# The k maxima of an attention block taken by VectorE block transposes and a DRAM scratch instead of TensorE transposes

## The chip, the cores and the metric

The kernel runs on one core of one Trainium2 chip. The core has a matrix engine (TensorE, "PE" in the profile; its weight loads are the row "PEld"), a vector engine (VectorE, "DVE"), a scalar engine (ScalarE, "ACT"), GpSimd ("POOL"), and SyncE ("SP"), whose queue issues most of the transfers here. The metric is the device time of one execution in microseconds (us), as the median over several runs.

## What is computed

An attention of the softmax-separated kind feeds a two-layer block. `softmax` over the head dimension of q, softmax over the sequence of k, then two products:

```python
# q, k, v: [8 batches, 8 heads, 576, 64] float32
k_s = k - np.max(k, axis=2, keepdims=True)      # maximum over the sequence, one for each (b, h, d)
k_s = np.exp(k_s)
k_s = k_s / (np.sum(k_s, axis=2, keepdims=True) + 1e-09)
kv = np.einsum('bhsd,bhse->bhde', k_s, v)
x = np.einsum('bhsd,bhde->bhse', q_s, kv)       # q_s: the same softmax of q over its last axis
# x as [4608, 512]; w_in [512, 2048], w_out [2048, 512]
h = x @ w_in
r = np.maximum(h, 0.0)
out = (s * (r * r) + b) @ w_out
```

The change bears on `np.max(k, axis=2)`. The sequence lies over the partitions in this kernel, so that maximum goes across partitions.

## The kernel before

The rows of x are worked in nine blocks of 512 (eight batches' first 512 tokens, and a ninth block of the 64 left over of each batch). A block is 16 *steps*, one for each 128 columns of the hidden layer; there are 144. Step t has two halves on TensorE: 12 matmuls of 128x512 that make `h` (`h_parts`, line 600), and 12 that add to the output `acc` (`o_parts`, line 674), in three terms each, since each operand is split in a high and a low part. Between them stand four operations, ACT `r` (620), DVE `r` (621), ACT `gh` (622) and DVE `gl` (613), and the `acc` half of step t-1 is issued after the `h` half of step t (`LAG = 1`).

The attention is worked in 16 *pairs* of two head pairs (256 columns of x), two for each batch. Pairs 0 and 1 serve the first block, and pairs 2 and 3 the second; these four are laid out beside the first 16 steps, with an order worked out by a class of the kernel's own (`Order`). From step 16 on, each block computes the attention of the next batch beside its own steps: pairs 4 to 15, twelve in all. The generator `pair` (line 490) yields 13 times (`STAGES`), and `advance` (line 788) runs so many of its stages at each half step that two pairs are through by step 13 of a block (`UF`). A stage is then run at each half step, beginning half a step into the block; `kv` is the seventh.

In what order an engine takes its instructions is fixed when the program is built, by a list scheduler: it follows estimated durations, transfers included, and gives an engine, among the instructions that it holds ready, the one that stands first in the text. `held()` adds that an instruction may not go ahead of the last `gl` so far. On the chip each engine takes its queue in that fixed order and waits where an operand isn't there. SP's queue is such a queue too: a transfer that waits holds up those behind it.

A pair, in the text's order. `kt`, `qt` and `vt` are the raw k, q and v (`raws[0]`, one buffer, loaded anew by `loads(pr + 1)` when the pair's last reader is through). Of four heads of k, [128, 4, 5, 64], the maximum over the five row groups is taken on DVE (`k_max_2` 461, `k_max_1` 464 and 465) into `m1` [128, 4, 64]. `k_turn` (469) turns it with two TensorE transposes into PSUM (`kT`, tag `sm`, one buffer), `k_top` (472) reduces over the free axis on DVE to `km` [128, 2], and `spread` (476) spreads it back over all partitions with two more TensorE transposes, of a broadcast, into PSUM (`mb`). `k_less` (480) subtracts on DVE and `k_exp` (487, 488) takes the exponential on ACT and clears the unused rows on POOL. Then q's maximum (520), subtraction on POOL (521) and exponential (523); then `heads` (301), 40 small matmuls of k and v into `kv`, and their scaling; then twice normalisation, transposes (546) and product (563), whose result goes to the next block's x.

Of the kernel before, what the change touches and what calls it, by code (L numbers as in the profile page):

```python
# [8 lines left out]
F32 = mybir.dt.float32  # L9
# [5 lines left out]
ALU = mybir.AluOpType  # L15
AX = mybir.AxisListType
# [10 lines left out]
def attention_moe(ctx: ExitStack, tc: tile.TileContext, q, k, v, w_in, w_out, s, b, out):  # L27
    nc = tc.nc
    B, H, S, D = q.shape
    DM, FF = w_in.shape  # L30
    DO = w_out.shape[1]
    P = 128
    NP = H // 2
    NFC = FF // P
    NQ = 4
    LEFT = S - NQ * P
    NT = NQ + 1
    TB = NQ * P
    LAG = 1
    NTMP = 3  # L40
# [11 lines left out]
    work = ctx.enter_context(tc.tile_pool(name="work", bufs=1))  # L52
    small = ctx.enter_context(tc.tile_pool(name="small", bufs=4))
# [3 lines left out]
    dram = ctx.enter_context(tc.tile_pool(name="dram", bufs=1, space=bass.MemoryType.DRAM))  # L57
# [24 lines left out]
    def by_head(t):  # L82
        return t[:, 0:KQ].rearrange("p (h n d) -> p h n d", h=4, d=D)
# [4 lines left out]
    def v_tile(t):  # L88
        return t.rearrange("p (h n e) -> p h n e", h=4, n=NT)
# [16 lines left out]
    def held():  # L106

        return tc.issue_after(gls[-1].ins)
# [184 lines left out]
    def bc(t, shape):  # L293
        return t.unsqueeze(3).to_broadcast(shape)

    def heads(kv, kt, vt):

        for i in range(2):
            for n in range(NT):
                for h in range(2):  # L300
                    nc.tensor.matmul(  # L301
                        kv[h * D:(h + 1) * D, i], kt[:, i, h, n], vt[:, 2 * i + h, n], start=(n == 0), stop=(n == NT - 1)
                    )

    def scales(pr, z, src):

        nc.vector.tensor_scalar(z, src, 1e-9, None, op0=ALU.add)
        nc.vector.reciprocal(z, z)
        zr = small.tile([P, 2, 2], F32, name=f"zr_{pr}", tag="zr")
        nc.vector.tensor_tensor(out=zr, in0=own, in1=z.unsqueeze(2).to_broadcast([P, 2, 2]), op=ALU.mult)  # L310
        return zr

    def blocks(pr, kv, zr):
        kvf = kvfs[pr % 2]
        shape = [P, 2, 2, D]
        nc.vector.tensor_tensor(
            out=kvf, in0=kv.unsqueeze(2).to_broadcast(shape), in1=zr.unsqueeze(3).to_broadcast(shape), op=ALU.mult
        )
        return kvf
# [135 lines left out]
    def k_tiles(pr):  # L455
        m2 = work.tile([P, 4, 2, D], F32, name=f"m2_{pr}", tag="m2")
        m1 = work.tile([P, 4, D], F32, name=f"m1_{pr}", tag="m1")
        return m2, m1, small.tile([P, 2], F32, name=f"km_{pr}", tag="km")

    def k_max_2(kt, m2):  # L460
        nc.vector.tensor_tensor(out=m2, in0=kt[:, :, 0:2], in1=kt[:, :, 2:4], op=ALU.max)

    def k_max_1(kt, m2, m1):
        nc.vector.tensor_tensor(out=m1, in0=m2[:, :, 0], in1=m2[:, :, 1], op=ALU.max)
        nc.vector.tensor_tensor(out=m1[0:LEFT], in0=m1[0:LEFT], in1=kt[0:LEFT, :, NQ], op=ALU.max)

    def k_turn(m1, kT):
        for i in range(2):
            nc.tensor.transpose(kT[:, i * P:(i + 1) * P], m1[:, 2 * i:2 * i + 2].rearrange("p h d -> p (h d)"), ident)

    def k_top(kT, km):
        nc.vector.tensor_reduce(out=km, in_=kT[:, 0:2 * P].rearrange("p (u s) -> p u s", u=2), axis=AX.X, op=ALU.max)

    def spread(km, mb):
        for i in range(2):
            nc.tensor.transpose(mb[:, i * P:(i + 1) * P], km[:, i:i + 1].to_broadcast([P, P]), ident)  # L476
        return mb

    def k_less(kt, mb, i):
        nc.vector.tensor_tensor(  # L480
            out=kt, in0=kt,
            in1=mb[:, i * P:(i + 1) * P].rearrange("p (h d) -> p h d", h=2).unsqueeze(2).to_broadcast([P, 2, NT, D]),
            op=ALU.subtract,
        )

    def k_exp(kt):
        nc.scalar.activation(kt, kt, AF.Exp)  # L487
        nc.gpsimd.memset(kt[LEFT:P, :, NQ], 0.0)

    def pair(pr):  # L490
        us = (2 * pr, 2 * pr + 1)
        bb = us[0] // NP
        kt, qt, vt = tiles.pop(pr)
        kt, qt, vt = by_head(kt), by_head(qt), v_tile(vt)
        kts, qts = [[t[:, 2 * i:2 * i + 2] for i in range(2)] for t in (kt, qt)]

        def sm(n):
            return ps.tile([P, 512], F32, name=f"{n}_{pr}", tag="sm", bufs=1)

        m2, m1, km = k_tiles(pr)  # L500
        with held():
            k_max_2(kt, m2)
        k_max_1(kt, m2, m1)
        yield
        kT = sm("kT")
        k_turn(m1, kT)
        k_top(kT, km)
        yield
        mb = spread(km, sm("mb"))
        for i in range(2):  # L510
            k_less(kts[i], mb, i)
            k_exp(kts[i])
            yield

        qes = []
        for i in range(2):
            u, qt = us[i], qts[i]
            qm = small.tile([P, 2, NT], F32, name=f"qm_{u}", tag="qm")
            with held():
                nc.vector.tensor_reduce(out=qm, in_=qt, axis=AX.X, op=ALU.max)  # L520
            nc.gpsimd.tensor_tensor(out=qt, in0=qt, in1=bc(qm, [P, 2, NT, D]), op=ALU.subtract)  # L521
            qe = work.tile([P, NT, 2, D], F32, name=f"qe_{u}", tag="qe", bufs=2)
            nc.scalar.activation(qe.rearrange("p n h d -> p h n d"), qt, AF.Exp)  # L523
            qes.append(qe)
            yield

        kv = sm("kv")[:, 0:2 * (D + 1)].rearrange("p (u e) -> p u e", u=2)
        heads(kv, kt.rearrange("p (u h) n d -> p u h n d", u=2), vt)
        kvf = blocks(pr, kv[:, :, 0:D], scales(pr, small.tile([P, 2], F32, name=f"z_{pr}", tag="z"), kv[:, :, D]))
        kvhl = work.tile([P, 2, 2, 2 * D], F32R, name=f"kvhl_{pr}", tag="m2")  # L530
        split(kvf.rearrange("p u h d -> p u (h d)"), kvhl[:, 0], kvhl[:, 1], nc.scalar.copy, nc.gpsimd)
        yield
        def normalize(i):
            u, qe = us[i], qes[i]
            qs = small.tile([P, NT, 2], F32, name=f"qs_{u}", tag="qs")
            nc.vector.tensor_reduce(out=qs, in_=qe, axis=AX.X, op=ALU.add)  # L536
            nc.vector.tensor_scalar(qs, qs, 1e-9, None, op0=ALU.add)
            qr = small.tile([P, NT, 2], F32, name=f"qr_{u}", tag="qr")
            nc.vector.reciprocal(qr, qs)  # L539
            nc.gpsimd.tensor_tensor(out=qe, in0=qe, in1=bc(qr, [P, NT, 2, D]), op=ALU.mult)  # L540

        def transpose(i):
            u, qe = us[i], qes[i]
            qT = ps.tile([P, 1024], F32, name=f"qT_{u}", tag="big")
            for n in range(NT):
                nc.tensor.transpose(qT[:, n * P:(n + 1) * P], qe[:, n, :, :].rearrange("p h d -> p (h d)"), ident)  # L546
            qh = work.tile([P, S], F32R, name=f"qh_{u}", tag="qh")
            ql = work.tile([P, S], F32R, name=f"ql_{u}", tag="ql")
            split(qT[:, 0:S], qh, ql, nc.scalar.copy, nc.vector)
            terms = ((kvhl[:, 0, i], qh), (kvhl[:, 0, i], ql), (kvhl[:, 1, i], qh))  # L550
            return terms

        def product(i, terms):
            u = us[i]
            hp = u % NP

            HB = TB // 2
            xh, xl = x_tile(bb)
            xp = ps.tile([P, 2, 512], F32, name=f"xp_{u}", tag="big")
            halves = [xp[:, 0], xp[:, 1]]  # L560
            for a, (t, src) in enumerate(zip(halves, (slice(0, HB), slice(HB, S)))):
                for j, (lhs, rhs) in enumerate(terms):
                    nc.tensor.matmul(  # L563
                        t[:, 0:src.stop - src.start], lhs, rhs[:, src], start=(j == 0), stop=(j == len(terms) - 1)
                    )
                if a == 1:
                    keep_left(u, t[:, HB:HB + LEFT])
            hl = [t[:, hp, :].rearrange("p (a c) -> p a c", a=2) for t in (xh, xl)]
            split(xp[:, :, 0:HB], hl[0], hl[1], nc.scalar.copy, nc.vector)

        for i in range(2):
            normalize(i)
            yield
            t = transpose(i)
            yield
            product(i, t)
            yield
# [121 lines left out]
    NU = B * NP  # L699
    NBLK = B + 1  # L700
    NSTEP = NBLK * NFC
    STAGES = 13
    tiles = {}

    def transfers():
# [74 lines left out]
    def due(t):  # L780

        blk, f = divmod(t, NFC)
        return NP // 2 * STAGES * (blk - 1 + min(1.0, f / UF))

# [54 lines left out]
```

## Time and profile before

| | |
|---|---|
| median of 3 runs | 901.12 us (900.09 to 901.48) |
| the profiled execution | 900.48 us |
| its span, first to last instruction | 898.7 us |
| TensorE busy | 876.0 us, 97% |
| VectorE busy | 459.5 us, 51% |
| ScalarE busy | 357.4 us, 40% |
| GpSimd busy | 83.6 us, 9% |
| granted TensorE clock, mean | 0.997 |
| chain that ended last | TensorE 89%, of it `h` 41%, `acc` 41% |

The times in the rows below are of the profiled execution. It took 1.8 us more than its span, which is the time around the first and the last instruction. A row of an engine is busy time; a matmul's duration includes its way through the array, so that consecutive matmuls overlap, and what one adds to the time is read from the distance of starts. A granted clock of 1.00 is the full 2.4 GHz of TensorE. A wait that ends on another engine's instruction names it behind an arrow.

### The profile page before, as it was taken

To read this page: it belongs to the slowest core of one execution; us is meant where nothing else is said; L and a number is where in the kernel's file an instruction comes from. 1 tells how busy PE (TensorE), PEld (TensorE's weight loads), DVE (VectorE), ACT (ScalarE), POOL (GpSimd) and SP (SyncE) were. 2 spreads that over 40 slices of the span, in tenths; PEclk is the share of its full clock that TensorE was granted. 3 is DMA by queue.
4 is the path that set the end of the run, shared out by engine and by line. 5 is a ranking of instruction groups with operands and counts; after the bars stand their busy time and mean duration, and the time that the engine had idled before them with its cause. 6 is when DMAs were issued, how large, how long until landed. Compare 5 with 4: busy or idle time off the path is not lost.

```text
span 898.7 us, 11364 instructions
## 1 busy us (share of the span) xinstructions
PE 876.0 (97%) x4528; PEld 721.8 (80%) x4528; DVE 459.5 (51%) x723; ACT 357.4 (40%) x564; POOL 83.6 (9%) x110
## 2 busy tenths in 40 slices
PE   4899999999999999999999999999999999999997
PEld 3577778888888888888888888888888888888886
DVE  6999975563364536353636345554545332223222
ACT  5999863342233333242334333333333322222222
POOL 1000001110020202020102002110202100000000
PEclk9999999999999999999999999999999999999999
DMA  9977211303130303030130213031300110001001
GB/s 241 305 258 240 72 39 50 80 5 81 47 80 4 80 19 109 5 80 3 48 79 18 69 47 80 4 80 47 83 4 1 50 47 1 1 1 47 1 1 47
DMA packets 82308, 57.35 MB, mean 64 GB/s; under 512 B 52944, under 2 KB 77520, under 8 KB 82128
## 3 DMA queue, kind: packets, MB, share of 16 engines
q1 hardware_dynamic: 80848, 55.52, 21.7%
q10 hardware_dynamic: 1408, 1.12, 0.4%
q8 instruction: 35, 0.57, 0.3%
q14 instruction: 17, 0.14, 0.1%
HBM read 46.14 MB, written 10.49 MB: 63 GB/s over the span
## 4 chain that ended last, share of the span: by engine, by line
PE 89%; DVE 4%; ACT 3%; DMA 2%; SPq 1%; issue 1%; ACTq 0%; DVEq 0%
PE h L600 41%; PE acc L674 41%; PE xp L563 2%; PE kv L301 2%; PE qT L546 1%; ACT low L202 1%; DMA raw<-in_q_dram 1%; DVE w L225 1%; ACT st L205 1%; DMA k<-in_k_dram 1%; PE xp L443 0%; DMA q<-in_q_dram 0%; ACT r L633 0%; DVE low L218 0%; DVE st L215 0%
## 5 line engine op out<-in xcount | busy, mean ns | idle before, releaser
L600 PE MATMUL h<-x,w 128*128 128x512 f32 x1728 | 428.9, 393 | 2.3 <-ACT r L633 1.6
L600 PEld LDWEIGHTS h<-x,w 128*128 128x128 f32 x1728 | 321.9, 188 | 70.5 <-ACT r L633 3.4
L674 PE MATMUL acc<-w,gh 128*128 128x512 f32 x1152 | 340.6, 392 | 0.0
L674 PEld LDWEIGHTS acc<-w,gh 128*128 128x128 f32 x1152 | 215.1, 188 | 44.3 <-ACT o L687 0.4
L621 DVE SCALAR_TENSOR_TENSOR r<-r,sb 128x512 f32<-128x512 f32 x128 | 102.0, 797 | 277.2 <-ACT r L620 277.1
L674 PE MATMUL acc<-w,gl 128*128 128x512 f32 x576 | 207.7, 392 | 0.5 <-DVE gl L643 0.5
L620 ACT ACTIVATE r<-h 128x512 f32<-128x512 f32 x128 | 76.5, 597 | 302.6 <-PE h L600 293.0
L613 DVE SCALAR_TENSOR_TENSOR gl<-r,sb,gh 128x512 fp32r<-128x512 f32 x132 | 102.6, 777 | 84.6 <-ACT gh L622 84.2
L622 ACT ACTIVATE gh<-r,sb 128x512 fp32r<-128x512 f32 x128 | 92.7, 724 | 94.3 <-DVE r L621 93.6
L674 PEld LDWEIGHTS acc<-w,gl 128*128 128x128 f32 x576 | 108.1, 188 | 23.7 <-DVE gl L643 1.4
L521 POOL TENSOR_TENSOR q<-q,qm 128x640 f32<-128x640 f32 x24 | 30.3, 1262 | 442.6 <-DVE qm L520 441.3
L540 POOL TENSOR_TENSOR qe<-qe,qr 128x640 f32<-128x640 f32 x24 | 30.6, 1275 | 49.2 <-DVE qr L539 45.0
L487 ACT ACTIVATE k<-k 128x640 f32<-128x640 f32 x28 | 20.4, 736 | 20.1 <-DVE k L480 20.1
L523 ACT ACTIVATE qe<-q 128x640 f32<-128x640 f32 x24 | 17.5, 731 | 21.9 <-POOL q L521 21.9
L536 DVE TENSOR_REDUCE qs<-qe 128x10 f32<-128x640 f32 x24 | 19.6, 817 | 12.7 <-ACT qe L523 12.7
L480 DVE TENSOR_TENSOR k<-k,mb 128x640 f32<-128x640 f32 x28 | 21.9, 816 | 7.3 <-PE mb L476 7.3
L102 DVE TENSOR_TENSOR x<-xp,x 128x512 fp32r<-128x512 f32 x24 | 16.6, 690 | 16.9 <-ACT x L101 16.9
L102 DVE TENSOR_TENSOR ql<-qT,qh 128x576 fp32r<-128x576 f32 x24 | 18.2, 757 | 11.6 <-ACT qh L101 11.6
L563 PE MATMUL xp<-qh,kvhl 128*128 128x256 f32 (+1 forms) x96 | 23.4, 297 | 0.0
L101 ACT CAST qh<-qT 128x576 fp32r<-128x576 f32 x24 | 15.4, 641 | 18.7 <-PE qT L546 18.7
L301 PEld LDWEIGHTS kv<-v,k 128*64 128x64 f32 x600 | 19.4, 141 | 4.2 <-issue 2.0
L301 PE MATMUL kv<-v,k 128*64 128x65 f32 (+1 forms) x600 | 21.4, 228 | 0.0
(101 smaller groups left out, 519.8 us busy)
## 6 DMA issues: line engine op xcount, KB each, us to landing
st<-in_moe_w_in_dram SPq DMA_DIRECT2D x16, 512.0 KB, 7.7
st<-in_moe_w_out_dram SPq DMA_DIRECT2D x16, 512.0 KB, 8.5
out_dram<-o SPq DMA_DIRECT2D x16, 512.0 KB, 2.7
q<-in_q_dram SPq DMA_DIRECT2D x14, 512.0 KB, 4.6
k<-in_k_dram SPq DMA_DIRECT2D x14, 512.0 KB, 5.0
v<-in_v_dram SPq DMA_DIRECT2D x56, 128.0 KB, 4.7
xleft<-xleft SPq DMA_DIRECT2D x16, 64.0 KB, 1.7
xleft_all<-xleft SPq DMA_DIRECT2D x1, 1024.0 KB, 4.7
```

Source lines behind the costliest of these rows:

```text
L102: return eng_l.tensor_tensor(out=l, in0=src, in1=h.bitcast(F32), op=ALU.subtract)
L301: nc.tensor.matmul(kv[h * D:(h + 1) * D, i], kt[:, i, h, n], vt[:, 2 * i + h, n], start=(n == 0), stop=(n == NT - 1))
L480: nc.vector.tensor_tensor(out=kt, in0=kt, in1=mb[:, i * P:(i + 1) * P].rearrange("p (h d) -> p h d", h=2).unsqueeze(2).to_broadcast([P, 2, ...
L521: nc.gpsimd.tensor_tensor(out=qt, in0=qt, in1=bc(qm, [P, 2, NT, D]), op=ALU.subtract)
L540: nc.gpsimd.tensor_tensor(out=qe, in0=qe, in1=bc(qr, [P, NT, 2, D]), op=ALU.mult)
L563: nc.tensor.matmul(t[:, 0:src.stop - src.start], lhs, rhs[:, src], start=(j == 0), stop=(j == len(terms) - 1))
L600: nc.tensor.matmul(hp_, w[:, j, c, :], x[:, c, :], start=(c == 0 and i == 0), stop=(c == NP - 1 and i == 2))
L613: gls.append(nc.vector.scalar_tensor_tensor(out=gl, in0=r, scalar=b_col, in1=gh.bitcast(F32), op0=ALU.add, op1=ALU.subtract))
L620: nc.scalar.activation(r, hp_, AF.Relu)
L621: nc.vector.scalar_tensor_tensor(out=r, in0=r, scalar=s_col, in1=r, op0=ALU.mult, op1=ALU.mult)
L622: nc.scalar.activation(gh, r, AF.Identity, bias=b_col)
L674: last = nc.tensor.matmul(a, g[:, js], w_, start=(f == 0 and i == 0), stop=(f == NFC - 1 and i == 2)).ins
```

## The change

From step 16 on (pairs 4 to 15) the maximum over the partitions is found in another way. `k_max_0` takes the maximum over the row groups as before, but writes `m1` with the 64 columns of a head in the order even, odd. `k_out` transposes `m1` in blocks of 32x32 on DVE, reduces each block over its 32 columns on DVE, which leaves `top` [128, 4, 2] (for each group of 32 partitions the maxima of its own rows), and writes that to a DRAM scratch `maxima`, 4 KB, in pieces of 8 bytes. `k_in` reads the whole scratch into each of the 128 partitions (512 KB in all) in a tile `mb` of tag `tmp`, three buffers which the output tiles `o` use too. `k_join` takes the maximum over the four groups of partitions with two DVE operations (512 and 256 elements per partition), and `k_under` subtracts as `k_less` did, from SBUF instead of PSUM. Both transfers are issued by SP. The two q stages now stand ahead of `k_join`, the pair has 12 stages, and `kv` is the sixth. The four TensorE transposes and their reduction from PSUM are gone from pairs 4 to 15; pairs 2 and 3, before step 16, keep them.

```diff
--- before.py
+++ after.py
@@ -487,6 +487,42 @@
         nc.scalar.activation(kt, kt, AF.Exp)
         nc.gpsimd.memset(kt[LEFT:P, :, NQ], 0.0)
 
+
+    maxima = {}
+
+    def k_max_0(pr, kt):
+
+        m2, m1, _ = k_tiles(pr)
+        k_max_2(kt, m2)
+        m2s, ks = [t.rearrange("p h n (r t) -> p h n t r", t=2) for t in (m2, kt)]
+        m1 = m1.rearrange("p h (t r) -> p h t r", t=2)
+        nc.vector.tensor_tensor(out=m1, in0=m2s[:, :, 0], in1=m2s[:, :, 1], op=ALU.max)
+        nc.vector.tensor_tensor(out=m1[0:LEFT], in0=m1[0:LEFT], in1=ks[0:LEFT, :, NQ], op=ALU.max)
+        return m2, m1
+
+    def k_out(pr, m2, m1):
+        m = m2.rearrange("p h n d -> p (h n d)")[:, 0:4 * D]
+        nc.vector.transpose(out=m, in_=m1.rearrange("p h t r -> p (h t r)"))
+        top = small.tile([P, 4, 2], F32, name=f"top_{pr}", tag="top", bufs=1)
+        nc.vector.tensor_reduce(out=top, in_=m.rearrange("p (h t c) -> p h t c", h=4, t=2), axis=AX.X, op=ALU.max)
+        maxima[pr] = dram.tile([4, P, 2], F32, name=f"maxima_{pr}", tag="maxima", bufs=2)
+        nc.sync.dma_start(maxima[pr].rearrange("h p t -> p h t"), top)
+
+    def k_in(pr):
+        mb = work.tile([P, 4, 4, D], F32, name=f"mb_{pr}", tag="tmp", bufs=NTMP)
+        src = maxima.pop(pr).rearrange("h p t -> (h p t)").partition_broadcast(P)
+        nc.sync.dma_start(mb.rearrange("p h a d -> p (h a d)"), src)
+        return mb
+
+    def k_join(mb):
+        mb = mb.rearrange("p h a d -> p h (a d)")
+        for n in (2 * D, D):
+            nc.vector.tensor_tensor(out=mb[:, :, 0:n], in0=mb[:, :, 0:n], in1=mb[:, :, n:2 * n], op=ALU.max)
+        return mb[:, :, 0:D]
+
+    def k_under(kt, mb):
+        nc.vector.tensor_tensor(out=kt, in0=kt, in1=mb.unsqueeze(2).to_broadcast([P, 2, NT, D]), op=ALU.subtract)
+
     def pair(pr):
         us = (2 * pr, 2 * pr + 1)
         bb = us[0] // NP
@@ -497,20 +533,11 @@
         def sm(n):
             return ps.tile([P, 512], F32, name=f"{n}_{pr}", tag="sm", bufs=1)
 
-        m2, m1, km = k_tiles(pr)
         with held():
-            k_max_2(kt, m2)
-        k_max_1(kt, m2, m1)
+            m2, m1 = k_max_0(pr, kt)
+        k_out(pr, m2, m1)
         yield
-        kT = sm("kT")
-        k_turn(m1, kT)
-        k_top(kT, km)
-        yield
-        mb = spread(km, sm("mb"))
-        for i in range(2):
-            k_less(kts[i], mb, i)
-            k_exp(kts[i])
-            yield
+        mb = k_in(pr)
 
         qes = []
         for i in range(2):
@@ -522,6 +549,11 @@
             qe = work.tile([P, NT, 2, D], F32, name=f"qe_{u}", tag="qe", bufs=2)
             nc.scalar.activation(qe.rearrange("p n h d -> p h n d"), qt, AF.Exp)
             qes.append(qe)
+            yield
+        mb = k_join(mb)
+        for i in range(2):
+            k_under(kts[i], mb[:, 2 * i:2 * i + 2])
+            k_exp(kts[i])
             yield
 
         kv = sm("kv")[:, 0:2 * (D + 1)].rearrange("p (u e) -> p u e", u=2)
@@ -699,7 +731,7 @@
     NU = B * NP
     NBLK = B + 1
     NSTEP = NBLK * NFC
-    STAGES = 13
+    STAGES = 12
     tiles = {}
 
     def transfers():
```

## Rows read from the trace of the kernel before

**Rows 1.** Page, busy time, share and instructions of each engine.

```profile
PE 876.0 (97%) x4528; PEld 721.8 (80%) x4528; DVE 459.5 (51%) x723; ACT 357.4 (40%) x564; POOL 83.6 (9%) x110
```

**Rows 2.** Windows of 50 us: busy us (instructions) by engine, clock, DMA share, GB/s.

```profile
200.00:250.00 50.00, 50.00 (x264) 41.74 (x265) 21.20 (x35) 15.93 (x26) 2.11 (x3) 1.00 0.21 59
...
650.00:700.00 50.00, 50.00 (x271) 41.77 (x271) 23.57 (x40) 17.68 (x30) 6.14 (x7) 1.00 0.01 3
```

**Rows 3.** Chain that ended last, by time: start us, us, what; one pair's k.

```profile
238.20 2.72 PE h L600 x12
...
243.65 0.22 PE kT L469 x2
243.87 2.76 PE h L600 x12
...
248.90 0.22 PE mb L476 x2
...
249.58 2.72 PE h L600 x12
252.30 2.72 PE acc L674 x12
255.02 1.32 PE kv L301 x40
```

**Rows 4.** The same chain, the next pair's k.

```profile
281.13 2.73 PE h L600 x12
...
292.51 2.73 PE h L600 x12
```

**Rows 5.** Groups by line and shape: busy us, mean ns | idle before us.

```profile
L461 DVE TENSOR_TENSOR m<-k 128x512 f32<-128x512 f32 x14 | 9.6, 689 | 2.8 <-PE xp L563 2.8
...
L469 PE MATMUL kT<-ident,m 128*128 128x128 f32 x28 | 5.3, 272 | 0.0
```

**Rows 6.** Timeline of the pair of rows 3: start us, us, engine, line.

```profile
240.55 0.42 DVE L465 TENSOR_TENSOR m<-m,k 64x256 f32<-64x256 f32 x1
...
243.90 0.42 DVE L472 TENSOR_REDUCE km<-kT 128x2 f32<-128x256 f32 x1
...
248.84 0.75 DVE L613 SCALAR_TENSOR_TENSOR gl<-r,sb,gh 128x512 fp32r<-128x512 f32 x1 [0.79 <-ACT gh L622]
...
250.24 1.54 DVE L480 TENSOR_TENSOR k<-k,mb 128x640 f32<-128x640 f32 x2
...
252.36 0.72 ACT L487 ACTIVATE k<-k 128x640 f32<-128x640 f32 x1
...
253.98 0.20 POOL L488 MEMSET k<- 64x128 f32 x1
...
254.72 0.39 SPq L274 DMA_DIRECT2D q<-in_q_dram  x1
```

**Rows 7.** Timeline at the late scratch, written and read back: start us, us.

```profile
705.80 0.37 SPq L244 DMA_DIRECT2D xleft<-xleft  x1
...
707.53 0.33 SPq L800 DMA_DIRECT2D xleft_all<-xleft  x1
...
713.74 0.60 ACT L620 ACTIVATE r<-h 128x512 f32<-128x512 f32 x1 [3.29 <-PE h L600]
714.23 2.17 ACT L101 CAST x<-xleft_all 128x512 fp32r<-128x512 f32 x4
```

**Rows 8.** DMA issues by line: count, KB each, median us from issue to landing.

```profile
st<-in_moe_w_in_dram SPq DMA_DIRECT2D x16, 512.0 KB, 7.7
...
q<-in_q_dram SPq DMA_DIRECT2D x14, 512.0 KB, 4.6
...
xleft<-xleft SPq DMA_DIRECT2D x16, 64.0 KB, 1.7
xleft_all<-xleft SPq DMA_DIRECT2D x1, 1024.0 KB, 4.7
...
sb<-in_moe_s_dram ACTq DMA_DIRECT2D x1, 0.5 KB, 4.9
```

## The prediction

> **What bounds the kernel now.** I read the page's busy shares first: TensorE is busy 97% of the span, VectorE 51%, ScalarE 40%, GpSimd 9% [rows 1]. A share is an average, so next the windows: in every 50 us from step 16 on that hold attention work TensorE is busy for all 50 us, at a granted clock of 1.00, which is the 2.4 GHz level, while VectorE is at 21 to 24 us of 50 and the DMA engines at a fifth or less [rows 2]. So in the stretch that the change touches there is no wait on TensorE to win; what goes or comes there is its own work, and every wait that the change brings to TensorE is paid in full. The list of waits has no line for TensorE's matmuls in this stretch. Last the chain that ended last, in order of time: it runs along TensorE without a break, 2.72 us for each 12 matmuls, and the two pairs of transposes of a k stage lie on it [rows 3].
>
> **The change part by part.** *Removed from TensorE.* In the chain two transposes `kT` take 0.22 us, and two `mb` 0.22 us [rows 3], not the 272 ns that a row gives for one, since they overlap [rows 5]. To count the seams too I take distances: without insertions a step is 2 x 2.72 = 5.44 us; from the `h` at 243.87 on to that at 249.58, with the `mb` transposes in between, it is 5.71, and from 238.20 to 243.87, with `kT`, 5.67 [rows 3], so 0.27 + 0.23 = 0.50 us a pair. The next pair gives the same: 292.51 - 281.13 = 11.38 for two steps, less 10.88, 0.50 [rows 4]. The bare pieces make the lower bound, 0.44. Twelve pairs: 12 x 0.50 = 6.0 us (5.3 by the bare pieces). Pairs 2 and 3 keep theirs.
>
> *On VectorE.* The maxima over row groups stay (three operations). Removed is the reduction out of PSUM, 0.42 us [rows 6]. Added are the block transpose, the reduction and the two operations of `k_join`. No 32x32 transpose is in this trace; the nearest rows have 256 elements a partition like it, 0.42 for a maximum and for a reduction [rows 6], and I take 0.42; at worst 0.69, the row with 512 elements [rows 5], at best 0.2. The reduction is 0.42, `k_join` 0.69 + 0.42. In all 1.5 us more for each pair, 18 us over the kernel, on an engine with half its time free. What hides it is the distance between `gl` and the matmuls that read it: `gl` ends at 249.59 [rows 6], its `acc` begins at 252.30 [rows 3], so 2.7 us. The subtraction stays 0.77 us each, from SBUF now; I take no change.
>
> *The two transfers.* SP has to issue the write, wait for its landing, and issue the read. The kernel has one such sequence already: the left-over rows are written to a scratch and read back. There the write was issued at 705.80, the read at 707.53, as soon as the write had landed [rows 7]; median landing is 1.7 us for 64 KB, and 4.7 for the read of 1 MB [rows 8]. The new write is 4 KB in 512 pieces of 8 bytes, against 256 pieces of 256 bytes there. I take that nearest row, 1.7 us; twice as much, 3.4, if pieces cost and not bytes; and at the far end 4.9, the smallest transfer of the trace [rows 8], which landed among the crowded loads of the start. The Trainium skill, DMA: Bandwidth & Descriptors, Specifications, speaks against the change here: below 512 bytes a transfer is off line rate and is done as read-modify-write. The 256-byte pieces at 1.7 us are below that limit too and show no such price; by the rule the write could be the 3.4 us. The read is 512 KB in pieces of 4 KB: from the two scratch rows, (4.7 - 1.7)/(1024 - 64) KB x 448 KB + 1.7 gives 3.1 us with long pieces; the loads of q, 512 KB in pieces of 1 KB, take 4.6; I take 3.6, nearer to the longer pieces. Far end: 7.7, the weights of the crowded start [rows 8]. The other queues: the only transfers behind SP's wait are the next pair's loads, which begin after q's exponentials, at 254.72 before [rows 6], and are read a block's half later; the output's stores are ahead.
>
> *Does `kv` still find its k?* From the end of `m1` at 240.97 [rows 6]: transpose and reduction 0.84, up to 0.75 for an `r` between them; `top` is there at some 242.2. Write 1.7, read 3.6: 247.5. `k_join` 1.1, with up to 0.75 of another operation ahead: 249.0. Two subtractions 1.54, the second exponential 0.72, the clearing on GpSimd 0.2 [rows 6]: about 251.5. Before, the clearing ended at 254.18 [rows 6] and `kv` began at 255.02 [rows 3]. So the chain is not later than before by these values. With a write of 3.4 and a read of 4.6 it is 254.2, the same as before; with both far ends 258.8.
>
> But the place of `kv` in TensorE's queue is not kept: the scheduler puts it where by its own estimates k is ready. If the chip is later than that, TensorE stands still before `kv`, and nothing covers it. The trace has one test of how those estimates stand to the chip, the scratch's sequence. The four casts of `xleft_all` stand ahead of the step's `r` in the text, and the data landed at 707.53 + 4.7 = 712.2; yet `r`, which could start only at 713.74, was put ahead of them [rows 7]. So the plan held the data for not yet there at 713.7: it counted at least 7.9 us from the write's issue where the chip took 6.4. On the same measure the chip is early by 1.5 us, and for a read of half the size I count 1.0. So I forecast that `kv` waits little: cost nothing, and from the moment at which the two transfers take over 1 us more than the values taken, all of the excess, twelve times.
>
> The sum: 900.48 - 6.0 = 894.5 us for the profiled execution. The median of the runs is 901.12, 0.6 above it, so 895.1 for a median.
>
> **The rivals.** *A late broadcast (slower).* All 128 partitions read the same 4 KB. If that repeated read runs at half rate (3.1 becomes 1.7 + 2 x 1.4 = 4.5; from 3.6 some 5.5) and the 8-byte write takes 3.4, the sequence is 3.6 us longer than the 5.3 taken; the 1.0 of estimate covers part, and TensorE waits 2.6 us before each `kv`: 12 x 2.6 - 6.0 = +25, some 926 us. Half of that excess, 1.3 us a pair, gives 911. It decides from an excess of 1.5 us on: 1.0 of cover and the 0.5 gained. For it: no row shows a repeated read, or pieces so small outside the start. Against it: the engines are a fifth busy, and the scratch's sequence was earlier than planned. Chance 0.24. The Trainium skill, the same page, Latency and other measured facts, tells of copies at half rate where the partitions' streams are a large power of two apart, and infers that they fall on the same memory channels; reads of one address would by that be such a case. No run here shows it yet.
>
> *A wait that eats the gain.* An excess between 1.35 and 1.65 us, or a `kv` that the plan puts so close that it waits 0.35 to 0.65 us a pair anyway: 899 to 903 us. Chance 0.10.
>
> *The change doesn't do what it says.* The TensorE time given back could turn up elsewhere at once: VectorE, with 1.5 us more and `k_join` waiting in its queue ahead of `r` and `gl`, would hold up the `acc` half. That takes more than 2.7 us of delay at one step; the added operations are under 0.8 each, and only the waiting `k_join` could reach it, late enough for `kv` to wait as well. Without that, 0.03 for about 901 us.
>
> **How the numbers follow.** The forecast has 0.63: 894 to 899 us, its middle at small waits 895.1. About 0.2% (1.8 us) is what a measurement of this kernel can tell from no change; so faster 0.63, same 0.10 + 0.03 = 0.13, slower 0.24. The range reaches from 893.9, with all seams counted and nothing lost, over the unchanged cases into the late broadcast, to 905; beyond that I leave most of its 0.24, some 0.18.
>
> **What would show it.** After the change TensorE's instructions should be fewer by 48; its steps at a pair's start 5.44 us apart; in the windows it should stay at 50 of 50 us. VectorE's busy time should be 18 us higher. Write and read should land in 1.7 and 3.6 us, and `kv` should be preceded by matmuls without a gap. The forecast is wrong if TensorE's weight loads for `kv` wait on GpSimd or ScalarE for k, or VectorE's `k_join` waits on a transfer by over a microsecond; then the step that failed is the landing time or the plan's place of `kv`, and the wait times twelve should give the difference.

## The result, and the profile after

The changed kernel takes 902.54 us in the median of 12 runs (901.71 to 904.63). The kernel before, beside it on the same chips, takes 900.65 (899.92 to 901.48). The ratio is 1.0023 with an interval of 1.0015 to 1.0030: slower by 0.2%, where 895.1 and faster was forecast. The time lies inside the range given, and on the other side of no change. The profiled execution of after took 903.18 us, its span 901.1, against 900.48 and 898.7. Of the experiments below, one execution of number 5 (1255.94 us) and one of number 7 (2260.38) fell into a slow state and are left out of the times and ratios.

The page of after, first its busy time, share and instructions of each engine, then the chain that ended last by engine, then three groups (line, engine, operation, tiles, count | busy us, mean ns of one | idle us of the engine before them and what ended it), then the landing times in us of the two added transfers:

```profile
PE 873.4 (97%) x4480; PEld 716.1 (79%) x4480; DVE 476.5 (53%) x759; ACT 356.1 (40%) x564; POOL 86.8 (10%) x110
...
PE 85%; DVE 7%; DMA 4%; SPq 1%; ACT 1%; issue 1%; POOL 0%; ACTq 0%; DVEq 0%
...
L520 DVE TENSOR_TENSOR mb<-mb 128x512 f32<-128x512 f32 x12 | 8.3, 692 | 43.1 <-DMA mb<-maxima 43.1
L505 DVE STREAM_TRANSPOSE m<-m 128x256 f32<-128x256 f32 x12 | 5.3, 438 | 0.2
...
mb<-maxima SPq DMA_DIRECT2D x12, 512.0 KB, 4.7
...
maxima<-top SPq DMA_DIRECT2D x12, 4.0 KB, 4.1
```

The removal is there: 48 instructions fewer on TensorE than in [rows 1], and 2.6 us less busy time. VectorE has 17.0 us more, as forecast (18). But the share of TensorE in the last chain fell from 89% to 85%, and the two added transfers stand in it now, with 1% each. The write landed in 4.1 us where 1.7 was taken, the read in 4.7 where 3.6 was.

The windows of 50 us (busy us and instructions of PE, PEld, DVE, ACT, POOL, then the granted clock, DMA share, GB/s), as [rows 2]:

```profile
150.00:200.00 50.00, 47.30 (x270) 38.32 (x268) 27.22 (x47) 16.29 (x28) 7.83 (x11) 0.93 0.25 70
200.00:250.00 50.00, 50.00 (x230) 41.57 (x230) 23.22 (x36) 16.26 (x27) 4.70 (x4) 1.00 0.16 46
```

Between step 16 and the end of the attention almost all of the idle time of TensorE lies in one window, 150 to 200, and there the granted clock is 0.93 too; in the same window of the kernel before, TensorE is busy for all 50 us at 1.00. That window holds pair 4, the first of the twelve.

The two traces were then laid step against step: the start of each step's ACT `r` in one less that in the other, from one pair's end to the next. Steps 16 and 23, where pair 4 begins and ends, first before and then after:

```profile
139.76 0.60 ACT L620 ACTIVATE r<-h 128x512 f32<-128x512 f32 x1 [3.47 <-PE h L600]
...
180.90 0.60 ACT L620 ACTIVATE r<-h 128x512 f32<-128x512 f32 x1 [2.80 <-PE h L600]
...
139.44 0.60 ACT L652 ACTIVATE r<-h 128x512 f32<-128x512 f32 x1 [3.48 <-PE h L632]
...
186.84 0.60 ACT L652 ACTIVATE r<-h 128x512 f32<-128x512 f32 x1 [2.06 <-PE h L632]
```

Pair 4 became 6.26 us longer. Pair 11 became 0.16 longer, and all the others shorter: pair 5 by 0.54, 6 by 0.22, 7 by 0.25, 8 by 0.44, 9 by 0.38, 10 by 0.26, 12 and 13 by 0.82 together, 14 by 0.44 and 15 by 0.35. With 0.32 gained ahead of step 16 that sums to +2.4 us, the difference of the spans. (Ahead of step 16 the profiled executions of all versions differ from before by -0.97 to +0.87 us, so those 0.32 us say nothing of the change.) So the question has two parts: what happens in pair 4, and why the others gain less than the 0.50 forecast.

The list of waits of after between 140 and 890 us (engine, line, what it waited for: us in total, times, longest); before, that list has no line for TensorE's matmuls:

```profile
DVE mb L520 <- DMA mb<-maxima: 43.1, 12, 4.4
ACT k L487 <- DVE k L524: 43.0, 11, 7.7
```

The join stands in VectorE's queue and waits 3.6 us for its data at every pair. So the plan of the scheduler held the two transfers for up to some 3.6 us shorter than the chip makes them; if it has VectorE idle there too, for less.

The chain of after through pair 4, in order of time (start us, us, what):

```profile
148.05 0.34 DVE top L507
...
148.40 4.18 DMA maxima<-top
...
152.65 4.21 DMA mb<-maxima
...
156.89 0.69 DVE mb L520
...
158.14 1.70 DVE k L524
...
159.87 0.75 ACT k L487
...
160.66 1.35 PE kv L301 x20
162.01 0.73 PE h L632
162.73 1.28 PE kv L301 x20
164.02 4.17 PE h L632 x11
```

The chain of before at the same place, where `kv` stands behind step 20's `h` and not ahead of it:

```profile
158.36 2.72 PE h L600 x12
161.07 1.32 PE kv L301 x40
```

And some rows of the timeline of the same stretch (start us, us, engine, line, tiles, in brackets the idle time before it and what ended it), with the windows of two pieces of it:

```profile
144.69 1.26 POOL L548 TENSOR_TENSOR q<-q,qm 128x640 f32<-128x640 f32 x1 [40.78 <-ACT r L652]
144.72 1.78 DVE L653 SCALAR_TENSOR_TENSOR r<-r,sb 128x512 f32<-128x512 f32 x1
...
157.88 1.28 POOL L572 TENSOR_TENSOR qe<-qe,qr 128x640 f32<-128x640 f32 x1 [5.36 <-DVE qr L571]
158.14 2.43 DVE L524 TENSOR_TENSOR k<-k,mb 128x640 f32<-128x640 f32 x2
...
160.51 0.58 ACT L652 ACTIVATE r<-h 128x512 f32<-128x512 f32 x1
160.66 1.35 PE L301 MATMUL kv<-v,k 128*64 128x65 f32 x20 [2.51 <-ACT k L487]
...
160.60:164.00 3.40, 3.34 (x42) 2.67 (x42) 2.17 (x3) 2.27 (x5) 0.40 (x2) 0.50 0.17 40
164.00:168.20 4.20, 4.20 (x14) 3.35 (x13) 0.91 (x4) 0.40 (x1) 0.73 (x1) 0.63 0.75 205
```

What is to be seen: `top` is written from 148.40 on, and 8.5 us pass until the join can start. TensorE's queue has `kv` next, and it stood still for 2.51 us. ScalarE's queue has the first exponential of k ahead of step 19's `r`, whose `h` was through at some 154.8, so `r`, `gh`, `gl` and the `acc` half behind them wait for k as well. After the stop the granted clock is 0.50, the 1.2 GHz level, over 3.4 us, and 0.63, a part at that level, over the next 4.2. The 40 matmuls of `kv` and 12 of `h` behind the stop take 7.53 us (160.66 to 168.19) where they take 1.32 + 2.72 = 4.04 in [rows 3]: another 3.5 us, of which 1.7 fall on the last 11 of `h` (4.17 us instead of 11/12 of 2.72). Stop and clock together make 6.0 of the 6.26 us. In the kernel before, both exponentials of this pair stand behind that `r`. Besides pair 4 only pair 5 has its exponentials and its `kv` earlier in the queues than before; in the other ten pairs they stand where they stood, or later.

### The profile page after: what moved, and what is told of

Read it like the earlier page. It is cut to its first block, busy times and chain, and to the rows that moved or that the text cites. A ratio compares the mean times of both kernels' runs of the same rounds, so it can differ in the third digit from the quotient of the medians.

```text
span 901.1 us, 11336 instructions
## 1 busy us (share of the span) xinstructions
PE 873.4 (97%) x4480; PEld 716.1 (79%) x4480; DVE 476.5 (53%) x759; ACT 356.1 (40%) x564; POOL 86.8 (10%) x110
## 4 chain that ended last, share of the span: by engine, by line
PE 85%; DVE 7%; DMA 4%; SPq 1%; ACT 1%; issue 1%; POOL 0%; ACTq 0%; DVEq 0%
PE h L632 39%; PE acc L706 39%; PE kv L301 2%; PE xp L595 2%; PE qT L578 1%; DMA mb<-maxima 1%; DMA maxima<-top 1%; DVE w L225 1%; DMA raw<-in_q_dram 1%; PE xp L443 1%; DVE low L218 1%; DVE gl L645 1%; DMA k<-in_k_dram 1%; SPq L284 1%; DVE st L215 0%
## 5 line engine op out<-in xcount | busy, mean ns | idle before, releaser
L706 PE MATMUL acc<-w,gh 128*128 128x512 f32 x1152 | 344.2, 393 | 0.0
L653 DVE SCALAR_TENSOR_TENSOR r<-r,sb 128x512 f32<-128x512 f32 x128 | 99.9, 781 | 269.4 <-ACT r L652 269.3
L706 PE MATMUL acc<-w,gl 128*128 128x512 f32 x576 | 210.4, 392 | 1.2 <-DVE gl L675 0.9
L645 DVE SCALAR_TENSOR_TENSOR gl<-r,sb,gh 128x512 fp32r<-128x512 f32 x132 | 98.7, 748 | 66.9 <-ACT gh L654 66.1
L520 DVE TENSOR_TENSOR mb<-mb 128x512 f32<-128x512 f32 (+1 forms) x24 | 13.4, 558 | 43.4 <-DMA mb<-maxima 43.1
L572 POOL TENSOR_TENSOR qe<-qe,qr 128x640 f32<-128x640 f32 x24 | 32.8, 1366 | 33.2 <-DVE qr L571 33.2
L488 POOL MEMSET k<- 64x128 f32 x28 | 5.8, 206 | 160.2 <-ACT k L487 70.9
L524 DVE TENSOR_TENSOR k<-k,mb 128x640 f32<-128x640 f32 x24 | 19.5, 855 | 0.3
```

Of the source, the lines that this page charges most:

```text
L645: gls.append(nc.vector.scalar_tensor_tensor(out=gl, in0=r, scalar=b_col, in1=gh.bitcast(F32), op0=ALU.add, op1=ALU.subtract))
L653: nc.vector.scalar_tensor_tensor(out=r, in0=r, scalar=s_col, in1=r, op0=ALU.mult, op1=ALU.mult)
L706: last = nc.tensor.matmul(a, g[:, js], w_, start=(f == 0 and i == 0), stop=(f == NFC - 1 and i == 2)).ins
```

## The experiments

Theories named in the expectations: A, the loss sits in pair 4 and comes from its place in the queues; against it B and C, by which it is spread over all pairs, by the late transfers or by what the change adds otherwise. Two came later: D, the late landings of the 8-byte write cost the later pairs an amount that varies between executions; and A', the narrower form of A, that it is the order of VectorE's and ScalarE's queues where pair 4 begins.

**1. The change from pair 5 on.** Pair 4 keeps its TensorE transposes.

```diff
+    def new(pr):
+        return pr > NP
-        k_out(pr, m2, m1); yield; mb = k_in(pr)
+        if new(pr):
+            ... the changed head of the pair
+        else:
+            ... the head of before, with k_turn, k_top, spread, k_less
```

> The change is made from pair 5 on; pair 4, the first after step 16, keeps the four TensorE transposes. Theory A (one pair): pair 4 alone loses 6.0 us, because its kv stands half a step earlier in TensorE's queue than that of the later pairs, and the other eleven gain 0.3 to 0.5 us each; then this kernel takes some 896.3 us, faster than both. Theory B (all pairs pay): each pair loses 0.15 us to its two transfers; then it takes 902.3 us. Theory C (VectorE's 18 us more delay gl in every pair): about 902 us as well.

Measured: 900.26 us (897.62 to 903.33, 12 runs), ratio 1.0004 [0.9994, 1.0015]. The profiled execution is the fastest, 897.62. In it pair 4 stands as before (+0.05), pair 5 is longer by 1.13 (two waits of `kv`, 0.91 and 0.31), and six pairs gain 0.35 to 0.44. Pairs 11 and 15 gain nothing (+0.07 and +0.05). Without pair 4 the loss is gone, but so is most of the gain, and the executions spread over 5.7 us. A is right for pair 4 and isn't all.

**2. The change in pair 4 alone.** The same edit with `pr == NP`.

> The change is made in pair 4 alone; pairs 5 to 15 keep the TensorE transposes. Theory A: the whole loss of the first pair without the gains of the others, 900.65 + 6.0 = 906.6 us. Theories B and C: a twelfth of the 1.9 us, so 900.8 us.

Measured: 905.53 us (904.40 to 907.30), ratio 1.0056 [1.0043, 1.0069]. The profiled execution, 907.30, the slowest of the five, has pair 4 longer by 7.16, of which `kv` waits 3.08, and 4.85 us for 11 matmuls of `h` behind that stop, at a granted clock of 0.52 (164.3 to 169.1). One pair, with one write and one read, costs 5.0 us by the ratio, 5.5 by the medians: A holds for it, and the rivals that spread the loss fall as its explanation.

**3. The transfers left out.** The scratch is neither written nor read; the join takes a partition's own values instead of the four groups' maxima, so the subtrahend isn't the maximum over the sequence.

```diff
-        maxima[pr] = dram.tile([4, P, 2], F32, name=f"maxima_{pr}", tag="maxima", bufs=2)
-        nc.sync.dma_start(maxima[pr].rearrange("h p t -> p h t"), top)
-        nc.sync.dma_start(mb.rearrange("p h a d -> p (h a d)"), src)
-        mb = k_join(mb)
+        mb = k_join(mb, kt)
```

> Both transfers are left out: the block transpose and the reduction are done and their result is not used, and the two operations of the join read k itself, so what is subtracted is a partition's own maximum and not that over all partitions. TensorE's and VectorE's work is that of the changed kernel. If the removed TensorE work is worth what the prediction took, 900.65 - 6.0 = 894.6 us; by the bare pieces of the chain, 895.4. Theory A and B: somewhere there, since no wait for a transfer is left. Theory C: VectorE's added work still delays gl, 897 us or more.

Measured: 902.99 us (902.03 to 903.86), ratio 1.0031 [1.0019, 1.0043]; a miss for every theory. No matmul waited for k, and TensorE has no stop from pair 4 to 15. Two lines of its chain show what came instead:

```profile
284.75 0.61 PE kv L301 x14
285.36 2.94 PE acc L701 x12
```

Without the transfers the scheduler has k earlier, splits the `kv` of pairs 5 to 15 into two or three pieces, and lays them among the other matmuls. In three pieces a `kv` takes 0.61 + 0.49 + 0.62 = 1.72 us instead of 1.32, and 12 matmuls behind a piece 2.94 to 2.96 instead of 2.72. The pairs alternate between +0.8 (three pieces) and -0.3 us (two). The order on TensorE is another one, so this run does not price the transfers, and I draw nothing on them from it.

**4. The write in pieces of 32 bytes.** The scratch is laid out by partition, so that each of the 128 partitions writes one piece of 32 bytes instead of four of 8. The read moves as many bytes as before; the join reorders.

```diff
-        maxima[pr] = dram.tile([4, P, 2], F32, name=f"maxima_{pr}", tag="maxima", bufs=2)
-        nc.sync.dma_start(maxima[pr].rearrange("h p t -> p h t"), top)
+        maxima[pr] = dram.tile([P, 4, 2], F32, name=f"maxima_{pr}", tag="maxima", bufs=2)
+        nc.sync.dma_start(maxima[pr], top)
```

> All twelve pairs as in the change, but the scratch is laid out by partition, so that the write goes in 128 pieces of 32 bytes and not 512 of 8; the join puts the order right again. If the 4.1 us that the write took are a matter of the number of pieces, it should land in 2.0 us or less, k be there 2 us earlier in every pair, and pair 4's wait of 2.5 us before kv shrink to 0.5: some 898 us by theory A. If they are a fixed trip, the write still takes 4 us and the time stays at 902.5 us.

Measured: 899.17 us (897.53 to 901.92, 12 runs), ratio 0.9989 [0.9980, 0.9997]. The join's wait and the write's landing in its profiled execution (901.92, the slowest of the twelve), read as those of after, and a window behind the stops of pair 4:

```profile
DVE mb L519 <- DMA mb<-maxima: 17.8, 12, 3.5
...
maxima<-top SPq DMA_DIRECT2D x12, 4.0 KB, 1.4
...
164.00:168.20 4.20, 4.20 (x17) 3.27 (x13) 1.51 (x5) 0.41 (x1) 0.73 (x1) 0.59 0.84 220
```

The same 4 KB land in 1.4 us in the median, and VectorE waits 17.8 us for the read instead of 43.1. Pairs 6 to 15 now gain 0.35 to 0.44 each. Pair 4 still loses 5.56, of which pair 5 behind it makes up 1.23: step 18's `gl` stands behind the waiting join and the `acc` half waits 1.18 for it, `kv` waits 0.89 and 0.85, and 12 matmuls of `h` then take 4.53 us, at a granted clock of 0.59 (the last line). The write is the cause in the later pairs. In pair 4 the two transfers took 2.9 and 4.7 us in this execution, longer than in the median, so whether that pair has a cause of its own is left to experiments 10 and 11.

**5 and 9. Both: from pair 5 on, with pieces of 32 bytes.** The edits of 1 and 4 together, run on two chips.

> The change from pair 5 on (pair 4 keeps the TensorE transposes) and with the write in 128 pieces of 32 bytes. The spread of 898 to 903 us that the version from pair 5 on with 8-byte pieces showed is laid to late transfers (theory D: the landing times differ between executions, and the later pairs' kv waits in most of them). With the write landing in 1.5 us rather than 4.1, 11 pairs should gain 0.40 each without waits: 895.6 us, spread under 2 us. If the eleven pairs pay for something else (theory C: VectorE), it stays at some 900 us.

> The best version so far (the change from pair 5 on, the write in 128 pieces of 32 bytes) once more, for a profile of an ordinary execution. 895.8 us as before; in its trace no wait of TensorE before kv, and 0.40 us gained for each of pairs 5 to 15.

Measured: 895.78 us (895.75 to 897.17), ratio 0.9955 [0.9942, 0.9968], and 895.55 (895.24 to 897.21), ratio 0.9950 [0.9936, 0.9963]. The trace of the second is read. Its busy time by engine:

```profile
PE 871.1 (98%) x4484; PEld 715.8 (80%) x4484; DVE 475.8 (53%) x756; ACT 355.6 (40%) x564; POOL 87.9 (10%) x110
```

No matmul waits for k, the mean granted clock is 1.000, and each of eleven pairs gains 0.35 to 0.45, 0.40 in the mean. This version is faster than both kernels, and its two forecasts came out within 0.2 and 0.3 us. The two causes do not simply add: against the 1.0023 of the changed kernel, experiment 1 alone gains 0.19% and experiment 4 alone 0.34%, and both edits together 0.68 and 0.73% (each interval is about 0.1% to either side).

**6. The join held back in pair 4.** Three more stages before it, and `held()` around it, so that it cannot go ahead of step 19's `gl`; pieces of 8 bytes.

```diff
+        for _ in range(3 if pr == NP else 0):
+            yield
+        with held() if pr == NP else nullcontext():
-        mb = k_join(mb)
+            mb = k_join(mb)
```

> All twelve pairs as in the change, 8-byte pieces; in pair 4 alone the join is held behind step 19's gl, so that ScalarE's queue has step 19's r and gh ahead of k's exponentials (in the changed kernel the first exponential stands ahead of that r), and kv stands 0.67 step later. Theory A: pair 4's loss of 6.3 us is the queue order there, not the transfers' length as such, so 902.5 - 6.0 = 896.5 us in executions like the one profiled, and by theory D up to 900 us in the median. If pair 4 has to lose for another reason (the first pair behind the hand-made order), 902 us.

Measured: 903.11 us (901.25 to 905.52, 8 runs), ratio 1.0032 [1.0020, 1.0043]; pair 4 still loses 5.21. The chain (start us, us, what), and then windows of two pieces of it:

```profile
143.34 1.46 DVE qm L547 x2
...
145.76 1.75 DVE r L656
...
149.35 0.66 DVE gl L648
...
150.10 0.61 ACT r L655
...
150.75 4.61 PE h L635 x12
...
143.00:148.00 5.00, 4.31 (x18) 2.92 (x16) 4.96 (x7) 1.79 (x3) 2.66 (x2) 1.00 0.00 0
150.70:155.40 4.70, 4.65 (x14) 3.61 (x15) 3.31 (x6) 0.91 (x2) 2.84 (x2) 0.64 0.43 121
```

The stop at the join is gone, and another stands ahead of it. VectorE is busy for 4.96 of 5 us from 143 on: both maxima of q stand in its queue with the k maxima, an `r` that takes 1.75, the block transpose and q's sum, all ahead of step 17's `gl`, and step 18's `r` came so late that TensorE stood for 2.75 us before the next `h`. Again the granted clock falls behind the stop (0.64), and 12 matmuls take 4.61 us. The changed kernel has no stop at that place: the edit, with three more stages to run in the same steps, brought it. So the expectation failed, but whether the stop at the join is the whole of pair 4's loss is not tested by this run.

**7. Held back, and pieces of 32 bytes.**

> The same hold in pair 4 and the write in 128 pieces of 32 bytes, in all twelve pairs. With neither pair 4's stop nor late writes: 900.0 - 12 x 0.40 = 895.2 us, the best of all so far. By theory C 900 us.

Measured: 901.56 us (900.01 to 902.46), ratio 1.0012 [1.0003, 1.0021]; pair 4 +5.21 again, and pairs 5 to 15 gain 0.40 each in the mean without a wait. The stop ahead of the join is just as long (2.74 us), and it begins at 147.0, when the write is not yet issued (148.39): so in this form it has nothing to do with the pair's transfers.

**8. The kernel of 1 once more, for a second profile.**

> The version from pair 5 on with 8-byte pieces once more, for a second profile. Its first was of the fastest execution (897.6 us; the median is 900.3). Theory D: a slower execution shows longer landings and waits of TensorE before kv in pairs that had none; the sum of those waits is the difference.

Measured: 900.76 us in the profiled execution, the only one and on another chip, against 897.62 in experiment 1. Two of its waits:

```profile
PE acc L727 <- DVE gl L666: 2.4, 2, 1.4
...
PE kv L301 <- ACT k L487: 1.6, 2, 1.3
```

Pairs 5, 9 and 11 now lose 1.54, 1.36 and 0.91 (in the first profile 1.13, -0.38 and 0.07), and the others gain as before, or a little more (pair 15); these three make up 3.0 of the 3.1 us between the executions. D holds in the main: with pieces of 8 bytes the transfers land so late that a pair tips over or not, from one execution to the next. It is not the write alone: in pair 9 the write took 4.6 us here and 4.2 in the first profile, and the read 6.6 and 4.4. What makes a landing later in one execution than in another wasn't found.

**10. All twelve pairs, pieces of 32 bytes, pair 4 begins one step later.** Two empty stages ahead of its first; otherwise the kernel of experiment 4.

```diff
+        for _ in range(2 if pr == NP else 0):
+            yield
         with held():
             m2, m1 = k_max_0(pr, kt)
```

> All twelve pairs, the write in 128 pieces of 32 bytes, and pair 4 begins two stages, one step, later; its k's exponentials then stand behind step 19's gh and its kv 0.67 step later, as in the version with the held join, but its maxima, transposes and q's maxima no longer stand ahead of step 17's r and gl on VectorE. Theory A' (pair 4 loses to what stands ahead of the steps' own operations in the queues of VectorE and ScalarE): no stop, 900.0 - 12 x 0.40 = 895.2 us. If pair 4 must lose behind the hand-made order, 901 us.

Measured: 895.92 us (895.02 to 897.13), ratio 0.9953 [0.9940, 0.9967]. Its chain through pair 4:

```profile
155.11 2.72 PE acc L711 x12
157.83 2.72 PE h L637 x12
160.55 0.55 PE qT L583 x5
161.10 0.95 PE acc L711 x4
162.04 1.32 PE kv L301 x40
```

TensorE runs through without a break, `kv` stands behind step 20's `h` again, and pair 4 gains 0.39 like the rest. One step later is enough, as A' has it. But the transfers of pair 4 are shorter here too, 1.4 and 3.7 us, since the next q loads begin only 3.7 us behind the read; experiment 11 takes that apart.

**11. The same with pieces of 8 bytes.**

> The same later start of pair 4 with the change's 8-byte pieces. Theory A' takes 6 us off the changed kernel, and theory D leaves the later pairs' waits that the version from pair 5 on had: some 899 to 900 us, with executions from 896 to 903. If late landings cost nothing, 895.2 us.

Measured: 898.65 us (897.28 to 901.27, 11 runs), ratio 0.9985 [0.9975, 0.9995]. In pair 4 (start us, us, engine, line, tiles):

```profile
161.00 1.15 DVE L520 TENSOR_TENSOR mb<-mb 128x512 f32<-128x512 f32 x2 [5.88 <-DMA mb<-maxima]
...
163.62 1.20 PE L708 MATMUL acc<-w,gh 128*128 128x512 f32 x4 [1.73 <-ACT gh L656]
```

Pair 4 loses 1.59 instead of 6.26, one stop of 1.73 us before the `acc` half, whose `r` stands on VectorE behind the late join, and no fall of the clock behind it. Its transfers took 4.2 and 4.7 us, no shorter than in after (4.2 and 4.2). So what is gained here comes from the place in the queues and not from shorter transfers, and pair 4 has a cause of its own. The other pairs lie between -0.45 and +0.13 (12 and 13 together -0.86). Of the 0.70% between the ratios of the changed kernel (1.0023) and of experiment 10 (0.9953), 6.3 us, the later start alone gives 3.4, and the longer pieces on top of it 2.9. Taken in the other order, by experiment 4, the pieces give 3.1 and the later start 3.2.

## Why the prediction was wrong, step by step

*TensorE's own work: right in kind, the term too large.* 0.50 us a pair was forecast; undisturbed pairs gain 0.44 as the first of a block and 0.35 to 0.38 as the second, 0.40 in the mean, so 4.8 us over twelve instead of 6.0. In experiment 10, in which nothing waits, pairs 4 to 15 are 4.8 us shorter in the trace, and the time is 4.8 us shorter by the medians on the same chip (900.72), 4.2 by the ratio. The mean is below my lower bound of 0.44. The distances of the first steps gave the seams that went (up to the step behind `kv` the first pair of a block is shorter by 0.46), but the same work is interleaved otherwise now, and at the pair's end 0.44 and 0.36 are left. Which seams make the difference isn't shown.

*VectorE: right.* 17.0 us more where 18 was forecast; block transpose 0.44 and reduction 0.41 where 0.42 each was taken, the join 0.69 and 0.42 as taken. As a sum it is hidden everywhere but in pair 4. One reading behind it was too narrow: over all windows of 50 us from 150 on that hold attention work, before, VectorE is busy for 21 to 29 us and the DMA engines for up to 0.31, not the 21 to 24 and a fifth of the two rows shown; the window of pair 4, 150 to 200, has 28.80.

*The write: the first term that was mis-sized.* I took 1.7 us from the scratch of 64 KB [rows 8] because it was the nearest row, and named 3.4 "if pieces cost and not bytes". Measured, 4 KB in 512 pieces of 8 bytes took 4.1 us (2.9 to 4.7), with the last pair, beside which nothing else is loaded, at 4.1 as well; in 128 pieces of 32 bytes it took 1.4. That is above the 3.4 and below the far end of 4.9. The Trainium skill, DMA: Bandwidth & Descriptors, Specifications, warned of transfers below 512 bytes. Its direction was right, but 32-byte pieces are below that limit as well and took 1.4 us, so the limit alone doesn't give the price. Whether it is the number of pieces or their size that costs is not separated: both differ by four between the two writes.

*The read: right alone, wrong in company.* 3.6 us was taken. In after it lands in 3.4 when nothing follows it, in 4.1 to 4.9 with the next pair's q loads issued 0.4 us behind it, and in 4.7 to 5.6 where such a load stands between write and read. I had written that the only transfers behind SP's wait begin after q's exponentials; but the change itself moves the q stages ahead of the join, and with them those loads into the very stretch in which the read runs. A repeated read at half rate, the forecast's rival, isn't seen: alone it is faster than taken.

*The plan's estimate: the step that decided.* From the sequence of `xleft` [rows 7] I inferred that the plan holds transfers for 1.5 us longer than they are, and counted 1.0 of it as cover. In after the plan held this one for 3.6 us shorter (43.1 us of waiting in 12 joins; with long pieces 17.8). One sequence of 64 KB and 1 MB in long pieces says nothing of a plan for 4 KB in short ones. The sign was wrong. Write and read together took 8.8 us in the median where 5.3 was taken. By the forecast's rule, all of the excess beyond 1.0 us is paid twelve times, so that would have been 2.5 us a pair, some 924 us. That failed as well, on the other side: VectorE waited 3.6 us for the data in every pair, yet TensorE waited before `kv` by more than 0.2 us in pair 4 alone. What covered it elsewhere is the place of `kv`, which the plan left where it was or moved back in ten pairs, and moved forward in pairs 4 and 5. So that the time lies inside the range is luck: two errors of opposite sign.

*All pairs alike: the step that cost most.* I multiplied one pair, that of [rows 3], by twelve, and checked it on the next [rows 4]. Pair 4 is different: its stages begin where a block's output and the step operations meet in VectorE's queue, `kv` stands 3.5 steps into its block instead of some 4, half a step earlier than in the kernel before, and ScalarE has k's exponential ahead of `r`. It alone costs 5 us (experiment 2), and 0.4 is gained there if it starts one step later and the write has long pieces (experiment 10). More than half of its price in the profiled execution is the clock: behind the stop of 2.51 us `kv` and `h` took 3.5 us more than at the full clock. Experiments 2, 6 and 7 ran 11 or 12 matmuls of `h` behind stops of 2.7 to 3.1 us at a granted clock of 0.52 to 0.64, for 1.9 to 2.4 us more; experiment 4, behind three shorter stops, lost 1.8 in the same way (0.59). I had priced a wait by its length alone. So the step of the forecast that failed is "`kv` waits little: cost nothing", taken alike for twelve pairs: in pair 4 `kv` waits 2.51 us, and stop and clock cost 6.0.

*"The subtraction: no change."* 0.77 us each holds where GpSimd is at rest. Beside GpSimd's product in pair 4 the two took 2.43 us together. In the kernel before, with the subtrahend in PSUM, the two took 1.55 in the same pair, though GpSimd's subtractions of q ran beside the first:

```profile
153.62 2.48 POOL L521 TENSOR_TENSOR q<-q,qm 128x640 f32<-128x640 f32 x2 [49.34 <-DVE qm L520]
...
155.28 1.55 DVE L480 TENSOR_TENSOR k<-k,mb 128x640 f32<-128x640 f32 x2 [1.15 <-PE mb L476]
```

I hadn't asked what runs on GpSimd at that time.

*The rivals.* The slower side came true, by another mechanism than mine: not a broadcast at half rate in all twelve pairs (+10 or more), but a stop in one, beside a late write. "A wait that eats the gain" describes the later pairs of experiments 1 and 8 well. The third, to which I gave 0.03, named a path that does occur: `gl` behind a waiting `k_join` held up the `acc` half by 1.2 us in experiment 4, and by 1.4 and 0.9 in experiment 8.

What stays open: which instruction in VectorE's and ScalarE's queues at the start of pair 4 is the dearest (the later start moves them all), why the two transfers, with 8-byte pieces, land later in one execution than in another and tip some pairs, and where the missing 0.1 us of a pair lies.

## What to carry to other kernels

Price a small transfer by its pieces: a scratch laid out so that each partition writes one piece made the write three times as fast here. The join that puts the order right costs no more by itself (0.69 and 0.42 us in both layouts); its first operation took 922 ns in the mean of experiment 4 instead of 692, because more of them fall beside a GpSimd operation there. When a saving is multiplied by a number of rounds, look at the first round by itself, since its neighbours in the queues are others: one stop of 2.5 us there, with the lowered clock behind it, cost more than all the other rounds saved. Where a scheduler's estimate stands between the change and the chip, take its sign from a transfer of the same shape or take none.

## What the runs showed of the hardware

- The same 4 KB from 128 partitions landed in DRAM in 4.1 us as 512 pieces of 8 bytes (median of after, 2.9 to 4.7) and in 1.4 us as 128 pieces of 32 bytes (median of experiment 4, up to 2.9).
- A 4 KB region read into each of 128 partitions, 512 KB, landed in 3.4 us alone, and in up to 5.6 us (after) and 6.6 (experiment 8) with loads of 512 KB in the same queue around it.
- VectorE's `r`, with two inputs in SBUF, took 1.78 us beside a GpSimd operation instead of 0.75, while that operation kept its 1.26. The Trainium skill, GPSIMD Engine Reference, says in its Specifications, that the two engines share SBUF interfaces, with contention for VectorE instructions with two SBUF inputs; the size of it here is these 1.0 us.
- After stops of TensorE of 2.5 (after), 2.7 (experiments 6 and 7) and 3.1 us (2), and after three of 1.2, 0.9 and 0.9 close together (4), the granted clock was 0.50 to 0.64 over the windows of three to five us read behind them, a part or all of it at 1.2 GHz instead of 2.4. In experiment 8, with stops of up to 1.4 us, the mean clock stayed at 0.999, and behind the stop of 1.7 us in experiment 11 it did not fall.
